# GpSimd makes the first shifted copy of VectorE's exponentials, a fifth key tile for VectorE, LN statistics tile by tile

## The chip, the cores and the metric

One core of a Trainium2 chip runs the whole program. The metric is the device time of one execution in microseconds: 1539.59 as the median of 3 runs (1539.48 to 1539.63).

## The reference

Two layers of attention and MLP with residuals, on x of 2048 rows by 512 columns in bf16; 32 heads of 16 columns, MLP width 1792. Both layers use the same weights.

```python
def _A_ref(x, wqkv, wo):                      # H = 32, Dh = 16
    qkv = (x @ wqkv).reshape(B, S, 3, H, Dh).transpose(2, 0, 3, 1, 4)
    q, k, v = qkv[0], qkv[1], qkv[2]
    scores = jnp.einsum("bhqd,bhkd->bhqk", q, k) * (Dh ** -0.5)
    p = softmax(scores, axis=-1)
    o = jnp.einsum("bhqk,bhkd->bhqd", p, v)
    return o.transpose(0, 2, 1, 3).reshape(B, S, D) @ wo

def _B_ref(x, w1, b1, w2, b2):
    return gelu(x @ w1 + b1) @ w2 + b2

x = x + _A_ref(layernorm(x), wqkv, wo)
x = x + _B_ref(layernorm(x), w1, b1, w2, b2)
x = x + _A_ref(layernorm(x), wqkv, wo)
x = x + _B_ref(layernorm(x), w1, b1, w2, b2)
```

## The kernel before, in words

**Cells.** The queries are taken in four chunks of 512. For one chunk and a group of four heads a *pass* goes over the 16 key tiles of 128 rows. One *cell* is the scores of one key tile, one head and 512 queries: a block of 128x512 in one PSUM bank. There are 2 layers x 32 passes x 16 tiles x 4 heads = 4096 cells. L1234 is their matmul; up to four cells of different heads run side by side in four row groups of TensorE. Its operand `qp` is a masked copy of Q that GpSimd makes (`qpad`, L1182).

**Two engines for exp.** ScalarE takes cells in batches of two or three banks and writes bf16 probabilities into units of the tile `pt`, a ring of PT_RING = 19 (`exps`, L1586). When the ring is full, parts of other tiles that are not in use are lent to it. VectorE takes cells only of the key tiles in KD, four for each layer. Its first pass (`dfirst`, L1386) scales and shifts the scores so that the bits of the uint16 result, read as bf16, approximate exp. Then `dchain` makes three more copies whose bits are shifted by 32, 64 and 96: per pair of cells L1461 writes copy one from copy zero (128x1024), and L1463 writes copies two and three from copies zero and one (128x2048). All four copies go into P·V (L1650), copies one to three against versions of V weighted by VW (`vc`, made by GpSimd in `vcopies`, L1165). So a cell of VectorE needs four P·V matmuls, a cell of ScalarE one. The pairs live in `du`, five buffers, with a sixth over a part of K in layer 1.

Which cells VectorE gets is decided while the program is planned: `attach` adds cells to a score batch where a bank is free, `swap` gives VectorE the third bank of a ScalarE batch when VectorE is less than 0.5 us behind. `next_d` hands out only cells of KD, of this pass and the next. The passes of the first chunk are split by key tiles: in layer 1 twelve passes first go over tiles 0 to 11, and later the same twelve over tiles 12 to 15.

**The rest, in the gaps.** Projections, output projection (`wo`), MLP (`hpair`, `gelu`, `ytile`) and LN run as background work between the cells, some of it released by the number of scores that have been done (`when`). LN takes its statistics on VectorE, rstd on GpSimd (L664, a power), the normalisation on GpSimd (L678, `xln`), and then a DMA transposes the tile (L682) into `xf` (for the MLP) or `xp` (for the next layer's projections). In the last segment LN is normalised on VectorE and transposed on TensorE. TensorE also runs *fillers* (L1222), matmuls whose results nobody reads, only in planned gaps.

**What sets the order.** `_Sched` plays the whole program forward on the host before it is emitted: each engine has a clock, each operation a cost in us, and the next operation of an engine is the ready one with the best priority. The emitted queues keep that order, with semaphore waits for every dependence; the engines then run at their own speed. Costs, latencies and priorities are thus only the plan, but a change of one number can reorder all that follows it. One part of the plan concerns GpSimd and VectorE: the copies of `dchain` are marked `port`, and the plan lets a marked VectorE operation that would begin inside one of the last four GpSimd operations begin only HOLD = 0.4 us later or at that operation's end:

```python
        if op.port and op.eng == "dve":
            at = max(t, self.clock["dve"])
            for a, b in self.pool_ops[-4:]:
                if a < at < b:
                    t = max(t, min(b, at + HOLD))
```

Of the kernel before, what the change touches and what calls it, by code (L numbers as in the profile page):

```python
# [5 lines left out]
ALU = mybir.AluOpType  # L6
# [12 lines left out]
NL = 2  # L19
# [1 line left out]
PVB = 6  # L21
MISC = (7, 5)
THIRD = 5
PT_RING = 19
LEND = (3, 2)
QP_RING = 3
W_RING = 4
# [6 lines left out]
LNP = 7  # L34
# [8 lines left out]
JB = 0.64  # L43
JS = 0.025
EARLY = 4
KD = ((4, 5, 6, 7), (0, 1, 2, 12))
NKD = 4
TAIL = 10
OPENING = 18
ROUNDS = 2  # L50
# [13 lines left out]
CPRIO = 8  # L64
FPRIO = 1.5
PVP = 2
PTURG = 6
DUURG = 1
# [2 lines left out]
DWIDE = 2  # L71
RWIDE = 2
AHEAD = 24
LOG2E = 1.4426950408889634
E_SCALE = 0.25 * LOG2E * 128
E_BIAS = 15992.765054484162
SHIFT = 32
# [128 lines left out]


OWN = 0.022
HOLD = 0.4
LATENCY = {"pe": 0.221, "act": 0.21, "dve": 0.139, "pool": 0.153328, "sp": 0.1}  # L210
OVERLAP = 0.083
ROUND = 1.02

# [1 line left out]
class _Sched:  # L215
# [76 lines left out]
    def _ready(self, op):  # L292
        t = 0.0
        for k in op.reads:
            if k not in self.P.lastw:
                return None
        for ev in self.P.deps(op.reads, op.writes):
            if op.eng == "pe" and ev[0] == "pe":
                continue
            t = max(t, self.end.get(ev, 0.0) - OWN * (op.eng == "dve" == ev[0]))  # L300
        if op.eng == "pe" and op.mode != self.mode:
            t -= SW
        if op.port and op.eng == "dve":
            at = max(t, self.clock["dve"])
            for a, b in self.pool_ops[-4:]:
                if a < at < b:
                    t = max(t, min(b, at + HOLD))
        return t
# [46 lines left out]
    def run(self):  # L355
        while True:
# [21 lines left out]
            for e, cand in best.items():  # L378
# [40 lines left out]
                self.clock[e] = at + MM  # L419
                self.end[ev] = at + MM + LATENCY[e]  # L420
            if e == "pool":
                self.pool_ops.append((start, start + cost))


SW = 0.107
# [111 lines left out]
class _Plan:  # L537
# [109 lines left out]
        yield from self.xmove(h, part(kept, h + 2), home, sem, ["KEPT.%d" % (h + 2)], keys)  # L647
        yield ("give", ("xin", 1, h + 2))

    def ln(self, tiles, dst, dkeys, prio, quick=False):  # L650

        T = self.T
        c, n = tiles[0], len(tiles)
        sl = slice(c, c + n)
        for t in tiles:
            yield ("need", ("xready", t, self.phase[t // 4]))
            yield _Op("dve", 0.66, lambda e, t=t: e.bn_stats(T["STATS"][:, t, :], T["X"][:, t % XT, :]),
                      reads=["X.%d" % (t % XT)], writes=["ST.%d" % t])
# [5 lines left out]
        yield _Op("pool", 0.25 + 0.33 * n, lambda e: e.tensor_tensor(  # L664
            out=T["RSTD"][:, sl], in0=T["VARR"][:, sl], in1=T["NHALF"][:, 0:n], op=ALU.pow),
            reads=["VARR.%d" % c, "NHALF"], writes=["RSTD.%d" % c])
        yield _Op("dve", 0.157, lambda e: e.scalar_tensor_tensor(
            out=T["NMR"][:, sl], in0=T["MV"][:, sl, 0], scalar=-1.0, in1=T["RSTD"][:, sl], op0=ALU.mult, op1=ALU.mult),
            reads=mvk + ["RSTD.%d" % c], writes=["NMR.%d" % c])
        for t in tiles:  # L670
            yield ("spawn", self.ln_tile(c, t, dst, dkeys, quick), prio)

    def ln_tile(self, c, t, dst, dkeys, quick):
        T = self.T
        ph = self.phase[t // 4]
        x = yield ("acq", "xln")
        eng, cost = ("dve", 0.4) if quick else ("pool", 1.0)
# [116 lines left out]
    def norm(self, l, seg, g, b, part, final):  # L794
# [35 lines left out]
        nb = w // 32  # L830
        for i, t in enumerate(ts):
            o3 = T["OTT"][:, o, 0:w].rearrange("p (k c) -> p k c", c=32)[:, :, 16 * t:16 * t + 16]
            yield _Op(*(("pool", 0.1 + 0.62 * w / 512) if pool else ("dve", 0.153 + 0.262 * w / 512)), lambda e, i=i, o3=o3: e.tensor_tensor(  # L833
                out=o3, in0=x3[:, i * nb:i * nb + nb, 0:16],
                in1=T["RC"][:, i * nb:i * nb + nb, None].to_broadcast([128, nb, 16]), op=ALU.mult),
                reads=["XT", "RC"], writes=["OTT.%d.%d" % (o, t)])
# [198 lines left out]
    def post(self, l, seg):  # L1035
# [7 lines left out]
        yield ("need", ("otn", l, seg, 3))  # L1043
        for t in tiles:
            yield ("spawn", self.wo(l, seg, t), 10)
        for t in tiles:
            yield ("need", ("xready", t, 2 * l + 1))
        yield ("give", ("ofree", l, seg))
        self.phase[c] = 2 * l + 1
        if prev:  # L1050
            yield ("need", ("xfree",) + prev)
        xf, xk = lambda t: T["XF"][:, :, (t % 4) * 128:(t % 4) * 128 + 128], lambda t: ["XF.%d" % (t % 4)]
        for ts in ([t] for t in tiles) if last else (tiles,):
            yield ("spawn", self.ln(ts, xf, xk, LNP, last), 0.2 if last else LNP)
        for t in tiles:
            yield ("need", ("lnt", t, 2 * l + 1))
        if prev:
# [10 lines left out]
        for i, t in enumerate(tiles):  # L1068
            yield ("cond", self.when(l, seg, yb + ys * i))
            yield ("spawn", self.ytile(l, seg, t), 13)  # L1070
        for t in tiles:
# [4 lines left out]
        self.phase[c] = 2 * l + 2  # L1076
        if prev:
            yield ("need", ("pfree",) + prev)
        xp, pk = lambda t: T["XP"][:, :, (t % 4) * 128:(t % 4) * 128 + 128], lambda t: ["XP.%d" % (t % 4)]
        yield ("spawn", self.ln(tiles, xp, pk, LNP), LNP)  # L1080
# [90 lines left out]
    def qpad(self):  # L1171
        T = self.T
        for pi, (l, seg, g, kts, part, final) in enumerate(self.pas):
# [5 lines left out]
            s = yield ("acq", "qp")  # L1179
            q = T["Q"][:, b, 512 * qc + q0:512 * qc + q0 + w]  # L1180
            for i, t in enumerate(ts):
                yield _Op("pool", 0.15 + 0.62 * w / 512, lambda e, s=s, q=q, i=i, t=t, w=w: e.tensor_scalar(  # L1182
                    T["QP"][:, s, w * i:w * i + w], q, T["MASK"][:, t:t + 1], 1.0, op0=ALU.mult, op1=ALU.mult),
                    reads=["Q.%d.%d" % (b, qc), "MASK"], writes=["QP.%d" % s])
            yield ("give", ("qp", pi), s)
# [263 lines left out]
    def dchain(self, pair):  # L1449
# [5 lines left out]
        if self.open is pair:  # L1455
# [5 lines left out]
        one = _Op("dve", 0.151 + 0.134 * n, lambda e: e.tensor_scalar(U[:, 1, 0:n, :], U[:, 0, 0:n, :], SHIFT, None, op0=ALU.add),  # L1461
                  reads=key[0], writes=key[1])
        two = _Op("dve", 0.152 + 0.266 * n, lambda e: e.tensor_scalar(U[:, 2:4, 0:n, :], U[:, 0:2, 0:n, :], 2 * SHIFT, None, op0=ALU.add),  # L1463
                  reads=key[0] + key[1], writes=key[2] + key[3])
        one.port = two.port = True
        yield one
        yield two
        self.duleft[du] = n
        for jj, (pi, kt, a) in enumerate(cells):
            l, seg, g = self.pas[pi][:3]  # L1470
# [2 lines left out]
            for i in range(4):  # L1473
                if i == 0:
                    ws, wk = [T["V"][l][:, kt, 8 * gb + 2 * a + t, 0:17] for t in ts], ["V%d.%d" % (l, kt), "V%d1" % l]
                else:
                    ws = [T["VC"][:, j, i - 1, 17 * h:17 * h + 17] for h in [8 * gb + 2 * a + t for t in ts]]
                    wk = ["VC.%d.%d" % (j, i - 1)]
                self.dq[(pi, a)].append((ws, U[:, i, jj, :].bitcast(BF16), wk + [key[i][jj]],
                                         ("du", du) if i == 3 else None, i == 3, kt))  # L1480

    def units(self, n):
        for lo, hi in self.blocks:
# [118 lines left out]
    def pvs(self):  # L1602
        T = self.T
        pools = self.s.pools
        for pi, (l, seg, g, kts, part, final) in enumerate(self.pas):
# [16 lines left out]
                return len(pools["du"]) <= DULOW and len(wide) >= DWIDE and any(self.dq[k] for k in cols)  # L1622

            def urge():
                return 0.5 if len(pools["pt"]) < PTURG or len(pools["du"]) < DUURG else PVP

            def build(op, start, pi=pi, b=b, l=l, cols=cols, begun=begun, n=n):
                op.fns, op.reads, rounds = [], [], 0
# [129 lines left out]
```

## Time and profile before

| | |
|---|---|
| median of 3 runs | 1539.59 us |
| the profiled execution's own time | 1540.0 us |
| its span (first to last instruction) | 1538.2 us |
| ScalarE busy | 1504.6 us, 98% |
| TensorE busy | 1452.2 us, 94% |
| VectorE busy | 1394.3 us, 91% |
| GpSimd busy | 202.9 us, 13% |
| TensorE clock granted | 1.00 |
| chain that ended last, by engine | ScalarE 64%, TensorE 23%, VectorE 12% |

A row of a group names the line, engine and operation, then output and input with shapes and the count; behind the first bar stand the us in which the group kept its engine busy and the mean ns of one instruction, behind the second the idle us just before them and who ended it. Rows of a table by stage give start:end, the length, then busy us and instruction count of PE, PEld, DVE, ACT and POOL, the clock, the DMA share and GB/s. A timeline row gives start, duration, engine, line, operation and count. Instructions of VectorE overlap a little at their ends, so the means of groups add up to more than the busy time. PE is TensorE, DVE VectorE, ACT ScalarE, POOL GpSimd.

### The profile page before, as it was taken

The page shows a single profiled execution, that of the slowest core. Times are in us where ns is not written, and L with a number is a line of the kernel's source. Part 1 is how long each engine was busy: PE and PEld are TensorE (multiplying, and loading weights), DVE is VectorE, ACT ScalarE, POOL GpSimd, SP SyncE. Part 2 cuts the span into 40 slices and gives each one's busy share as a digit, 9 for nine tenths or more (in the row PEclk, how much of TensorE's full clock was granted, in tenths as well). Part 3 has the DMA queues.
Part 4 walks back from the last instruction along what each step waited for, and adds up shares of the span by engine and source line. Part 5 has one row for each costly group of instructions (what it writes and reads, how often), then busy time and mean ns, then how long its engine had stood idle before and what let it go on. Part 6 is the DMA issues. An engine that isn't in the chain of part 4 may idle for free.

```text
span 1538.2 us, 46317 instructions
## 1 busy us (share of the span) xinstructions
PE 1452.2 (94%) x20352; PEld 445.9 (29%) x20352; DVE 1394.3 (91%) x2633; ACT 1504.6 (98%) x1377; POOL 202.9 (13%) x250
## 2 busy tenths in 40 slices
PE   8999899999999999999899999889999999999998
PEld 3222222222222222222222222222222222343344
DVE  6689999989999999989799899899989989999893
ACT  7999999999999999999999999999999999999996
POOL 5300002001020020100320011122002001010000
PEclk9999999999999999999999999999999999999999
DMA  5200001152111531215211431001153105312522
GB/s 145 50 2 1 2 3 42 36 166 84 33 39 50 162 74 36 49 57 157 58 50 43 133 100 46 16 1 36 36 159 91 37 21 163 114 37 69 167 65 64
DMA packets 145045, 103.39 MB, mean 67 GB/s; under 512 B 37069, under 2 KB 143822, under 8 KB 144846
## 3 DMA queue, kind: packets, MB, share of 16 engines
q1 hardware_dynamic: 144846, 100.44, 23.0%
q8 instruction: 162, 2.65, 0.7%
q14 instruction: 37, 0.30, 0.1%
HBM read 88.61 MB, written 4.19 MB: 60 GB/s over the span
## 4 chain that ended last, share of the span: by engine, by line
ACT 64%; PE 23%; DVE 12%; issue 1%; DMA 0%; ACTq 0%; DVEq 0%
ACT pt L1586 57%; PE ps L547 8%; PE ps L1234 7%; PE ps L1650 7%; DVE du L1386 5%; ACT g L986 3%; DVE du L1463 2%; DVE du L1461 1%; ACT kt L1586 1%; ACT v L1586 1%; ACT q L1586 1%; DVE g L965 1%; ACT L1586 1%; ACT L986 1%; DVE kt L1386 0%
## 5 line engine op out<-in xcount | busy, mean ns | idle before, releaser
L1586 ACT ACTIVATE pt<-ps 128x1024 bf16<-128x1024 f32 (+1 forms) x1239 | 1344.8, 1245 | 8.5 <-PE ps L1234 6.5
L1386 DVE TENSOR_SCALAR du<-ps 128x512 uint16<-128x512 f32 x893 | 596.3, 684 | 58.7 <-PE ps L1234 56.2
L1234 PE MATMUL ps<-qp,kt 32*128 32x512 bf16 x4096 | 529.3, 384 | 45.4 <-ACT pt L1586 31.6
L1650 PE MATMUL ps<-pt,v 128*17 128x512 bf16 (+1 forms) x3287 | 405.4, 359 | 13.2 <-ACT pt L1586 8.9
L1650 PE MATMUL ps<-du,vc 128*17 128x512 bf16 (+1 forms) x3000 | 354.5, 358 | 3.6 <-ACT pt L1586 2.0
L1463 DVE TENSOR_SCALAR du<-du 128x2048 uint16<-128x2048 uint16 x448 | 307.9, 694 | 1.7
L1234 PEld LDWEIGHTS ps<-qp,kt 32*128 32x128 bf16 x4096 | 137.4, 91 | 584.0 <-ACT pt L1586 239.9
L1182 POOL TENSOR_SCALAR qp<-q,mask 128x512 bf16<-128x512 bf16 (+1 forms) x91 | 70.9, 779 | 978.6 <-PE ps L1234 968.5
L1461 DVE TENSOR_SCALAR du<-du 128x1024 uint16<-128x1024 uint16 x448 | 183.1, 427 | 2.1
L1650 PE MATMUL ps<-du,v 128*17 128x512 bf16 (+1 forms) x1000 | 162.0, 359 | 7.1 <-DVE xt L823 2.8
L1658 PE MATMUL ps<-vc,zero 128*17 128x512 bf16 x774 | 158.6, 381 | 0.0
L1650 PEld LDWEIGHTS ps<-pt,v 128*17 128x17 bf16 x3287 | 98.9, 88 | 129.7 <-issue 72.9
L547 PE MATMUL ps<-xf,wr 128*32 128x512 bf16 (+1 forms) x1888 | 129.8, 364 | 1.7 <-DVE g L965 1.3
L547 PE MATMUL ps<-wr,g 128*32 128x512 bf16 x1600 | 117.9, 383 | 2.9 <-DVE du L1386 1.0
L1650 PEld LDWEIGHTS ps<-du,vc 128*17 128x17 bf16 x3000 | 95.0, 89 | 80.1 <-issue 43.0
L965 DVE TENSOR_SCALAR g<-ps,hb1t 128x512 bf16<-128x512 f32 (+1 forms) x112 | 79.7, 712 | 2.4 <-PE ps L547 2.4
L1222 PE MATMUL ps<-vc 128*32 128x512 bf16 x852 | 68.1, 382 | 0.9 <-DVE du L1386 0.7
L678 POOL TENSOR_SCALAR xln<-x,rstd,nmr 128x512 bf16<-128x512 bf16 x58 | 55.3, 956 | 41.5 <-DMA xf<-xln 15.0
L1650 PEld LDWEIGHTS ps<-du,v 128*17 128x17 bf16 x1000 | 41.7, 89 | 51.9 <-issue 18.1
L1386 DVE TENSOR_SCALAR kt<-ps 128x512 uint16<-128x512 f32 x81 | 55.5, 685 | 1.2 <-PE ps L1234 0.9
L1222 PE MATMUL ps<-vc,zero 128*17 128x512 bf16 x692 | 56.4, 382 | 0.0
L833 POOL TENSOR_TENSOR ott<-xt,rc 128x256 bf16<-128x256 f32 x42 | 32.2, 767 | 174.5 <-DVE rc L826 150.4
(90 smaller groups left out, 1077.4 us busy)
## 6 DMA issues: line engine op xcount, KB each, us to landing
wr<-in_B_w_dram SPq DMA_DIRECT2D x256, 256.0 KB, 2.8
wr<-in_A_wqkv_dram SPq DMA_DIRECT2D x24, 256.0 KB, 3.0
wr<-in_A_wo_dram SPq DMA_DIRECT2D x18, 256.0 KB, 3.1
x<-in_A_x_dram SPq DMA_DIRECT2D x7, 512.0 KB, 4.4
kept<-x SPq DMA_DIRECT2D x4, 512.0 KB, 2.9
x<-kept SPq DMA_DIRECT2D x4, 512.0 KB, 4.0
out_dram<-x SPq DMA_DIRECT2D x16, 128.0 KB, 2.8
g<-in_A_wqkv_dram SPq DMA_DIRECT2D x3, 512.0 KB, 5.5
```

The source lines that it names most:

```text
L547: return [lambda e, a=a: e.matmul(out[32 * a:32 * a + 32, :], lhsT=lhsT[:, 32 * a:32 * a + 32], rhs=rhs, start=start, stop=stop, tile_posi ...
L965: yield _Op("dve", 0.21 + n / 966, lambda e, fc=fc, pb=pb: e.tensor_scalar(T["G"][:, fc, q], pb, T["HB1T"][:, fc:fc + 1], None, op0=ALU.ad ...
L986: lambda e, g=g: e.activation(out=g, in_=g, func=ACT.Gelu_apprx_tanh), reads=gk, writes=gk, prio=2)
L1182: yield _Op("pool", 0.15 + 0.62 * w / 512, lambda e, s=s, q=q, i=i, t=t, w=w: e.tensor_scalar(T["QP"][:, s, w * i:w * i + w], q, T["MASK"] ...
L1222: fns.append(lambda e, o=o, w=w, a=a, m=m: e.matmul(o, lhsT=w, rhs=rhs, start=start, stop=start, tile_position=(0, m * a)))
L1234: return (lambda e: e.matmul(o, lhsT=lhsT, rhs=rhs, start=True, stop=True, tile_position=(32 * a, 0)), ["K%d.%d.%d" % (l, gb, kt // 4), "Q ...
L1386: yield _Op("dve", 0.682, lambda e: e.tensor_scalar(u, self.bank(b), E_SCALE, E_BIAS, op0=ALU.mult, op1=ALU.add), reads=["B.%d" % b], writ ...
L1461: one = _Op("dve", 0.151 + 0.134 * n, lambda e: e.tensor_scalar(U[:, 1, 0:n, :], U[:, 0, 0:n, :], SHIFT, None, op0=ALU.add), reads=key[0], ...
L1463: two = _Op("dve", 0.152 + 0.266 * n, lambda e: e.tensor_scalar(U[:, 2:4, 0:n, :], U[:, 0:2, 0:n, :], 2 * SHIFT, None, op0=ALU.add), reads ...
L1586: yield _Op("act", 0.065 + 0.4267 * n, lambda e, src=src, dst=dst: e.activation(out=dst, in_=src, func=ACT.Exp, scale=0.25), reads=["B.%d" ...
L1650: op.fns.append(lambda e, o=o, lhsT=q[0][0][m], rhs=q[0][1][:, n * m:n * m + n], a=a, st=st, sp=sp: e.matmul(o, lhsT=lhsT, rhs=rhs, start= ...
L1658: op.fns.append(lambda e, o=self.bank(b)[32 * a:32 * a + 17, :], rhs=rhs, a=a, st=not begun[a], sp=end: e.matmul(o, lhsT=T["ZERO"][:, 0:17 ...
```

## The change

*Copies.* In `dchain`, if the planned clock of GpSimd is at most PSHIFT = 2 us ahead of VectorE's, copy one becomes an add on GpSimd (`dpool`), and VectorE makes copies two and three as two instructions of 128x1024 straight from copy zero; otherwise VectorE does all as before. The pair is handed to P·V when all three have been planned.

*Key tiles.* KD has five tiles for each layer; `vc` grows by three copies of V, and the ring `pt` shrinks from 19 units to 15.

*LN.* The statistics are started as soon as a tile of the residual is there, ahead of the wait for `xf` or `xp` to be free; that wait now stands before the normalisation (`gate`). The LN behind the first layer's MLP works in two halves of two tiles.

*The plan.* HOLD falls to 0.06, and a GpSimd operation is planned longer by half of the time that it shares with a marked VectorE copy; costs of GpSimd operations and one latency change; P·V gets priority 0.3 when all scores are done.

```diff
-PT_RING = 19
+PT_RING = 15
-KD = ((4, 5, 6, 7), (0, 1, 2, 12))
-NKD = 4
+KD = ((4, 5, 6, 7, 8), (0, 1, 2, 12, 13))
+NKD = 5
+PSHIFT = 2
-HOLD = 0.4
-LATENCY = {"pe": 0.221, ...
+HOLD = 0.06
+EXTEND = 0.5
+LATENCY = {"pe": 0.219, ...
...
             if e == "pool":
-                self.pool_ops.append((start, start + cost))
+                self.pool_ops.append([start, start + cost, ev])
+            if e == "dve" and op.port and self.pool_ops:
+                last = self.pool_ops[-1]
+                both = min(start + cost, last[1]) - max(start, last[0])
+                if both > 0:
+                    last[1] += EXTEND * both
+                    self.clock["pool"] = last[1]
+                    self.end[last[2]] += EXTEND * both
...  # ln
-    def ln(self, tiles, dst, dkeys, prio, quick=False):
+    def ln(self, tiles, dst, dkeys, prio, quick=False, gate=None):
-        yield _Op("pool", 0.25 + 0.33 * n, ...
+        yield _Op("pool", 0.37 + 0.18 * n, ...
...
+        if gate:
+            yield ("need", gate)
         for t in tiles:
             yield ("spawn", self.ln_tile(c, t, dst, dkeys, quick), prio)
...  # post
         for t in tiles:
             yield ("spawn", self.wo(l, seg, t), 10)
+        self.phase[c] = 2 * l + 1
+        xf, xk = ...
+        gate = ("xfree",) + prev if prev else None
+        for ts in ([t] for t in tiles) if last else (tiles,):
+            yield ("spawn", self.ln(ts, xf, xk, LNP, last, gate), 0.2 if last else LNP)
         for t in tiles:
             yield ("need", ("xready", t, 2 * l + 1))
         yield ("give", ("ofree", l, seg))
-        self.phase[c] = 2 * l + 1
-        if prev:
-            yield ("need", ("xfree",) + prev)
-        ...
...
+        if l < NL - 1:
+            self.phase[c] = 2 * l + 2
+            xp, pk = ...
+            for ts in (tiles[:2], tiles[2:]):
+                yield ("spawn", self.ln(ts, xp, pk, LNP, gate=("pfree",) + prev if prev else None), LNP)
         for t in tiles:
             yield ("need", ("xready", t, 2 * l + 2))
...  # dchain
-        yield one
-        yield two
+        flat = [U[:, i, 0:n, :].rearrange("p j q -> p (j q)") for i in range(4)]
+        if self.s.clock["pool"] <= self.s.clock["dve"] + PSHIFT:
+            yield ("spawn", self.dpool(pair, flat, key, n), CPRIO)
+            for i in (2, 3):
+                op = _Op("dve", 0.151 + 0.134 * n, lambda e, i=i: e.tensor_scalar(flat[i], flat[0], SHIFT * i, None, op0=ALU.add),
+                         reads=key[0], writes=key[i])
+                op.port = True
+                yield op
+            yield ("cond", lambda: pair.get("copied"))
+        else:
+            one = ...  # as before
+            two = ...  # as before
+            yield one
+            yield two
...
+    def dpool(self, pair, flat, key, n):
+        yield _Op("pool", 0.15 + 0.536 * n, lambda e: e.tensor_scalar(flat[1], flat[0], float(SHIFT), 1.0, op0=ALU.add, op1=ALU.mult),
+                  reads=key[0], writes=key[1])
+        pair["copied"] = True
...  # pvs
-                return 0.5 if len(pools["pt"]) < PTURG or len(pools["du"]) < DUURG else PVP
+                return 0.3 if self.ended else 0.5 if len(pools["pt"]) < PTURG or len(pools["du"]) < DUURG else PVP
```

More of the change, by code (lines that the diff above doesn't have):

```diff
@@ L208 @@
 OWN = 0.022
-HOLD = 0.4
-LATENCY = {"pe": 0.221, "act": 0.21, "dve": 0.139, "pool": 0.153328, "sp": 0.1}
+HOLD = 0.06
+EXTEND = 0.5
+LATENCY = {"pe": 0.219, "act": 0.21, "dve": 0.139, "pool": 0.153328, "sp": 0.1}
 OVERLAP = 0.083
@@ L304, in _ready @@
             at = max(t, self.clock["dve"])
-            for a, b in self.pool_ops[-4:]:
+            for a, b, _ in self.pool_ops[-4:]:
                 if a < at < b:
@@ L663, in ln @@
                   reads=mvk, writes=["VARR.%d" % c])
-        yield _Op("pool", 0.25 + 0.33 * n, lambda e: e.tensor_tensor(
+        yield _Op("pool", 0.37 + 0.18 * n, lambda e: e.tensor_tensor(
             out=T["RSTD"][:, sl], in0=T["VARR"][:, sl], in1=T["NHALF"][:, 0:n], op=ALU.pow),
@@ L676, in ln_tile @@
         x = yield ("acq", "xln")
-        eng, cost = ("dve", 0.4) if quick else ("pool", 1.0)
+        eng, cost = ("dve", 0.4) if quick else ("pool", 0.77)
         yield _Op(eng, cost, lambda e: e.tensor_scalar(
@@ L832, in norm @@
             o3 = T["OTT"][:, o, 0:w].rearrange("p (k c) -> p k c", c=32)[:, :, 16 * t:16 * t + 16]
-            yield _Op(*(("pool", 0.1 + 0.62 * w / 512) if pool else ("dve", 0.153 + 0.262 * w / 512)), lambda e, i=i, o3=o3: e.tensor_tensor(
+            yield _Op(*(("pool", 0.63 * w / 512) if pool else ("dve", 0.153 + 0.262 * w / 512)), lambda e, i=i, o3=o3: e.tensor_tensor(
                 out=o3, in0=x3[:, i * nb:i * nb + nb, 0:16],
@@ L1045, in post @@
             yield ("spawn", self.wo(l, seg, t), 10)
+        self.phase[c] = 2 * l + 1
+        xf, xk = lambda t: T["XF"][:, :, (t % 4) * 128:(t % 4) * 128 + 128], lambda t: ["XF.%d" % (t % 4)]
+        gate = ("xfree",) + prev if prev else None
+        for ts in ([t] for t in tiles) if last else (tiles,):
+            yield ("spawn", self.ln(ts, xf, xk, LNP, last, gate), 0.2 if last else LNP)
         for t in tiles:
@@ L1048, in post @@
         yield ("give", ("ofree", l, seg))
-        self.phase[c] = 2 * l + 1
-        if prev:
-            yield ("need", ("xfree",) + prev)
-        xf, xk = lambda t: T["XF"][:, :, (t % 4) * 128:(t % 4) * 128 + 128], lambda t: ["XF.%d" % (t % 4)]
-        for ts in ([t] for t in tiles) if last else (tiles,):
-            yield ("spawn", self.ln(ts, xf, xk, LNP, last), 0.2 if last else LNP)
         for t in tiles:
@@ L1070, in post @@
             yield ("spawn", self.ytile(l, seg, t), 13)
+        if l < NL - 1:
+            self.phase[c] = 2 * l + 2
+            xp, pk = lambda t: T["XP"][:, :, (t % 4) * 128:(t % 4) * 128 + 128], lambda t: ["XP.%d" % (t % 4)]
+            for ts in (tiles[:2], tiles[2:]):
+                yield ("spawn", self.ln(ts, xp, pk, LNP, gate=("pfree",) + prev if prev else None), LNP)
         for t in tiles:
@@ L1075, in post @@
             return
[L1076 to L1080, printed above, removed]
         for t in tiles:
@@ L1181, in qpad @@
             for i, t in enumerate(ts):
-                yield _Op("pool", 0.15 + 0.62 * w / 512, lambda e, s=s, q=q, i=i, t=t, w=w: e.tensor_scalar(
+                yield _Op("pool", 0.27 + 0.42 * w / 512, lambda e, s=s, q=q, i=i, t=t, w=w: e.tensor_scalar(
                     T["QP"][:, s, w * i:w * i + w], q, T["MASK"][:, t:t + 1], 1.0, op0=ALU.mult, op1=ALU.mult),
@@ L1460, in dchain @@
         key = [["DU.%d.%d.%d" % (du, i, j) for j in range(n)] for i in range(4)]
[L1461 to L1465, printed above, removed]
-        yield one
-        yield two
+        flat = [U[:, i, 0:n, :].rearrange("p j q -> p (j q)") for i in range(4)]
[8 more added lines that the diff above has]
+        else:
+            one = _Op("dve", 0.151 + 0.134 * n, lambda e: e.tensor_scalar(flat[1], flat[0], SHIFT, None, op0=ALU.add),
+                      reads=key[0], writes=key[1])
+            two = _Op("dve", 0.152 + 0.266 * n, lambda e: e.tensor_scalar(U[:, 2:4, 0:n, :], U[:, 0:2, 0:n, :], 2 * SHIFT, None, op0=ALU.add),
+                      reads=key[0] + key[1], writes=key[2] + key[3])
+            one.port = two.port = True
+            yield one
+            yield two
         self.duleft[du] = n
@@ L1480, in dchain @@
                                          ("du", du) if i == 3 else None, i == 3, kt))
+    def dpool(self, pair, flat, key, n):
+        yield _Op("pool", 0.15 + 0.536 * n, lambda e: e.tensor_scalar(flat[1], flat[0], float(SHIFT), 1.0, op0=ALU.add, op1=ALU.mult),
+                  reads=key[0], writes=key[1])
+        pair["copied"] = True
     def units(self, n):
```

## The prediction

> **What bounds the kernel now.** I read the engine shares of the page first, then a table of three stages, then the costliest groups, the waits, and last the timeline where VectorE and GpSimd meet. From the page:
>
> ```profile
> PE 1452.2 (94%) x20352; PEld 445.9 (29%) x20352; DVE 1394.3 (91%) x2633; ACT 1504.6 (98%) x1377; POOL 202.9 (13%) x250
> ```
>
> The table by stage (opening, middle, closing; busy us of each engine):
>
> ```profile
> 0.00:77.00 77.00, 71.47 (x877) 21.83 (x877) 46.71 (x101) 68.70 (x70) 33.34 (x54) 1.00 0.37 97
> 77.00:1463.00 1386.00, 1311.57 (x17983) 387.51 (x17981) 1298.44 (x2425) 1375.97 (x1247) 165.85 (x191) 1.00 0.23 66
> 1463.00:1538.20 75.20, 69.17 (x1498) 36.54 (x1494) 49.17 (x109) 59.90 (x62) 3.71 (x5) 1.00 0.23 66
> ```
>
> In the middle ScalarE is busy 1375.97 of 1386 us (99.3%), VectorE 1298 (93.7%), TensorE 1312 (94.6%), at clock 1.00. ScalarE sets the pace; the time falls only where exponentials leave it. What they cost:
>
> ```profile
> L1586 ACT ACTIVATE pt<-ps 128x1024 bf16<-128x1024 f32 (+1 forms) x1239 | 1344.8, 1245 | 8.5 <-PE ps L1234 6.5
> L1386 DVE TENSOR_SCALAR du<-ps 128x512 uint16<-128x512 f32 x893 | 596.3, 684 | 58.7 <-PE ps L1234 56.2
> L1463 DVE TENSOR_SCALAR du<-du 128x2048 uint16<-128x2048 uint16 x448 | 307.9, 694 | 1.7
> L1461 DVE TENSOR_SCALAR du<-du 128x1024 uint16<-128x1024 uint16 x448 | 183.1, 427 | 2.1
> ```
>
> A cell (one 128x512 block of scores) goes to ScalarE (L1586) or to VectorE: a first pass from PSUM (L1386), then per pair of cells L1461 and L1463. With the `kt` rows VectorE has 893 + 81 = 974 of 4096 cells. The list allows 2 layers x 32 passes x 4 key tiles x 4 = 1024, so it is nearly used up. The waits of VectorE in the middle agree:
>
> ```profile
> DVE du L1386 <- PE ps L1234: 54.2, 71, 4.0
> ```
>
> 54 of its 88 idle us it waits for a cell to be given. A fifth tile raises the ceiling to 1280.
>
> The dispute is the copies. First VectorE, then GpSimd, in one window:
>
> ```profile
> 1280.04 0.69 DVE L1018 TENSOR_TENSOR x<-x,ps 128x512 bf16<-128x512 bf16 x1
> 1280.64 0.69 DVE L1386 TENSOR_SCALAR du<-ps 128x512 uint16<-128x512 f32 x1
> 1281.24 0.69 DVE L1463 TENSOR_SCALAR du<-du 128x2048 uint16<-128x2048 uint16 x1
> 1281.84 0.76 DVE L1461 TENSOR_SCALAR du<-du 128x1024 uint16<-128x1024 uint16 x2
> 1282.51 1.30 DVE L1463 TENSOR_SCALAR du<-du 128x2048 uint16<-128x2048 uint16 x2
> ```
>
> ```profile
> 1280.85 3.30 POOL L1182 TENSOR_SCALAR qp<-q,mask 128x256 bf16<-128x256 bf16 x2 [17.09 <-PE ps L1234]
> ```
>
> Instructions of 0.69 us start every 0.60 us, two copies of 128x1024 take 1282.51 - 1281.84 = 0.67, so 0.335 each. Meanwhile two GpSimd operations that take 0.48 each in undisturbed rows need 3.30: the row of copies keeps GpSimd out. The other way round:
>
> ```profile
> 1190.45 0.85 DVE L1461 TENSOR_SCALAR kt<-kt 128x1024 uint16<-128x1024 uint16 x1
> ```
>
> ```profile
> 1190.05 0.96 POOL L833 TENSOR_TENSOR ott<-xt,rc 128x256 bf16<-128x256 f32 x1 [1.47 <-DVE rc L826]
> ```
>
> A copy of 0.42 that begins inside a GpSimd operation takes 0.85. Counted over the whole trace: of 968 full copies 89 begin inside a GpSimd operation; 28 of them wait, 0.30 us on average, so 0.095 over all 89. Of the other 879 one is late.
>
> **Part by part.** All sums are for the middle stage, W = 1386 us; opening and closing (152 us) stay.
>
> *VectorE, before.* Two first passes and both copies: 2 x 0.60 + 0.335 + 0.60 = 2.135 us a pair, 1.07 a cell. 944 first passes start in the middle: 1008 us. The rest (residuals, bias, LN, norms) is 1298 - 1008 = 290.
>
> *VectorE, after.* Two separate 128x1024 copies replace one of 1024 and one of 2048: 2 x 0.60 + 2 x 0.335 = 1.87, a saving of 0.265 a pair, 0.935 a cell, before any wait. The wait is the unknown. GpSimd's 1024-column add stands in no row. Its q padding takes 0.48 at 256 columns and 0.69 at 512 when undisturbed, so 0.69 + 2 x 0.21 = 1.1 us; twice the 512 row is 1.4; I take 1.2. A blocked copy waited at most 0.43 behind the 0.69 operation, so about 0.94 behind this one. Bounds of the wait per pair: 0 (copies two and three follow the first pass on their own engine, GpSimd needs a semaphore and then queues behind them, as at 1280.85) and 0.94. GpSimd would be busy 203 + 500 x 1.4 = 900 us, 60%; two copies x 0.6 x 0.095 = 0.11, more for an operation twice as long. I take 0.15, near the low end, because the order within a pair favours VectorE. One pair in ten, where GpSimd is planned over 2 us late, stays at the old price. Cell: 0.9 x (0.935 + 0.075) + 0.1 x 1.07 = 1.016.
>
> The Trainium skill (SBUF — State Buffer, "Who interferes with whom") has a rule that speaks against the change: VectorE in a two-port mode and GpSimd hold the shared port pair for a whole instruction, and whoever issues second is fully blocked. The two windows above agree with it in both directions; the average of 0.095 says that it seldom falls on VectorE here. What it would cost is the second rival.
>
> *ScalarE.* In the middle it does 3823 - 944 = 2879 cells in 1323 us, 0.46 a cell; at 99.3% busy a moved cell is worth 0.463 of W.
>
> *The sum.* n cells go to VectorE, which reaches 96.5% (the best stages of 77 us reach 75 to 76, 98%; 34 of the 88 idle us are not for want of cells): n = (0.965 W - 290) / 1.016, W = 1386 - 0.463 (n - 944). This gives W = 1358, n = 1004: 60 cells more, 28 us less. Span 1538.2 - 28 = 1510. The profiled execution took 1540.0, 1.8 above its span, and the median is 0.4 lower: 1512.
>
> *TensorE.* A moved cell brings three more matmuls; 3788 of them on `du` cost 411 us in the middle, 0.109 each: 60 x 3 x 0.109 = 20 us, against 74 us idle and the fillers (L1222, 117 us of rows), which are placed only into gaps. Fewer ScalarE batches also mean fewer score rounds. I take nothing; without that cover 20 us.
>
> *GpSimd's queue.* The extra `vc` copies are 2 x 3 x 0.65 = 4 us; tile 8's V is written at 55.8, the first pair starts at 65.2. q padding and LN's `xln` now queue behind up to two or three adds, 2 to 4 us. q padding has waited 968 us in total for a buffer, so it is early. The first FFN matmul of a chunk follows its last `xln` by 5 to 7 us in the trace, so FFN, with the 58 transposes that SP's queue issues after `xln`, would come some 3 us later; it is background work, and no ScalarE batch in the middle waited for it. Nothing; 3 us if the last segment is held up by it.
>
> *LN.* The same 64 statistics, earlier and spread out on VectorE's queue; four groups become eight, with four more variance and `nmr` steps (0.19 and 0.15 us each, under 1.5 us of VectorE) and four more powers on GpSimd. At the end it could start 0.6 us sooner, but the chain there is TensorE's from 1514.5 to 1535.4. Nothing, or 0.6 gained.
>
> *Ring of 15 instead of 19.* ScalarE fills a unit in 0.46 us, so TensorE may lag 6.9 us, not 8.7. L1586 is idle 8.5 us in all, nearly all on scores, none seen for a unit. Nothing; up to 8 us if TensorE lags. The planner's new costs move every instruction a little; I bound that by the 10 us ScalarE idles in the middle, either way.
>
> **The rivals.**
>
> *The locks never meet.* VectorE alternates 1.2 us of first passes, which leave GpSimd alone (843 first passes without overlap and 131 with it both average 684 ns), and two copies; GpSimd's add fits into the first passes. Cell 0.935, VectorE 97.5%: W = 1326, time 1480. Against it: first passes and copies of several pairs come mixed, as above.
>
> *The lock turns on VectorE (slower).* GpSimd lags, its add for one pair still runs when the next pair's copies are due, and everything behind them on VectorE waits: first passes, so the third bank of a ScalarE batch. At half a hold, 0.47 a pair, a cell costs 1.17: W = 1402, time 1556. It decides from a wait of 0.35 a pair (cell 1.11, W = 1386). For it: 28 of 89, counted under a planner that puts a copy off by up to HOLD = 0.4 when GpSimd is planned busy, which the change lowers to 0.06; against it: VectorE starts first. With GpSimd always first, 0.94 a pair would give 1609 (an estimate). That is what the rule of the Trainium skill named above would make of this order; the windows shown hold both orders.
>
> *Copy one comes late to TensorE (slower).* It is done some 2 us after the first pass instead of 0.4; TensorE takes its queue in order, scores stand behind that matmul, ScalarE runs dry. If one pair in ten loses 0.8 us: 52 x 0.8 = 41, time 1553. It decides from 28 us over 517 pairs, 0.05 each.
>
> *The copies bring nothing, only the fifth tile does* (few adds reach GpSimd, or a wait of 0.27 eats the saving): cell 1.07, 96.5%: W = 1374, time 1527.
>
> **How the numbers follow.** Forecast 0.51 (its own range 1495 to 1524), locks never meet 0.17, tile alone 0.10, lock on VectorE 0.14, late copy 0.08. About 0.2% (3 us) is what a measurement of this kernel can tell from no change. Faster is the first three less 0.03 that would end within it, 0.75; slower is the last two less 0.01, 0.21; same 0.04. The range leaves out half of the best case and half of the two slower ones, some 0.2: 1482 to 1552.
>
> **What would show it.** Right: about 1030 first passes in all, GpSimd 50 to 65% busy with adds of 1.2 to 1.8 us, copies of 128x1024 at a mean of 0.43 to 0.50, VectorE at 94% of the whole span or more, ScalarE still at 98%. The lock: copies at a mean of 0.60 or more. The late copy: ScalarE idle above 60 us, and TensorE waiting on GpSimd's `du`. Tile alone: GpSimd under 40%. I am wrong if ScalarE's share falls below 96%, or if first passes stay under 990.

## The result, and the profile after

1630.97 us (median of 4 runs, 1626.4 to 1634.3) against 1539.53 before: ratio 1.059, 95% interval 1.0577 to 1.0602. The forecast was 1512, the range 1482 to 1552. The profiled execution took 1626.4 us, its span 1624.6.

The engine shares of the changed kernel's page:

```profile
PE 1472.5 (91%) x20210; PEld 441.8 (27%) x20210; DVE 1503.8 (93%) x2787; ACT 1507.6 (93%) x1374; POOL 797.1 (49%) x786
```

Its table by stage, with the middle lengthened by the 86 us that the span grew:

```profile
0.00:77.00 77.00, 71.77 (x916) 22.46 (x916) 46.78 (x102) 67.96 (x69) 38.08 (x60) 1.00 0.38 97
77.00:1549.00 1472.00, 1331.96 (x17810) 383.23 (x17806) 1402.02 (x2565) 1381.11 (x1245) 735.65 (x705) 1.00 0.22 62
1549.00:1624.60 75.60, 68.76 (x1496) 36.07 (x1488) 55.04 (x122) 58.56 (x62) 23.35 (x22) 1.00 0.23 67
```

Opening and closing are much as before. In the middle VectorE is busy 95.2% (93.7 before), ScalarE 93.8% (99.3 before). ScalarE no longer sets the pace, although it has fewer cells: the groups of the page show 961 + 87 = 1048 first passes instead of 974, and what the copies now cost:

```profile
L1611 ACT ACTIVATE pt<-ps 128x1024 bf16<-128x1024 f32 (+1 forms) x1110 | 1213.7, 1173 | 77.9 <-PE ps L1244 66.1
L1503 POOL TENSOR_SCALAR du<-du 128x1024 uint16<-128x1024 uint16 (+1 forms) x482 | 548.4, 1138 | 586.7 <-DVE du L1396 571.4
L1396 DVE TENSOR_SCALAR du<-ps 128x512 uint16<-128x512 f32 x961 | 635.9, 674 | 41.2 <-PE ps L1244 39.6
...
L1475 DVE TENSOR_SCALAR du<-du 128x1024 uint16<-128x1024 uint16 (+1 forms) x964 | 539.3, 586 | 2.8
```

A copy of 128x1024 takes 586 ns in the mean, not 427. The add (L1503) is at 1138 close to the 1.2 us that was assumed. And ScalarE now sits idle 66 us for scores (6.5 before). What the scores wait for, from the waits, before and after:

```profile
PEld ps L1234 <- ACT pt L1586: 239.9, 487, 1.9
...
PEld ps L1234 <- DVE du L1386: 116.4, 272, 1.1
```

```profile
PEld ps L1244 <- DVE du L1396: 231.9, 451, 1.6
...
PEld ps L1244 <- ACT pt L1611: 145.0, 309, 1.8
```

TensorE waits twice as long for a first pass of VectorE to free a bank, and less for ScalarE. The chain that ended last turns over with it: VectorE 73%, ScalarE 8% (12 and 64 before).

Where the copies lose the time, VectorE and then GpSimd in one window of the changed kernel's timeline:

```profile
533.33 1.28 DVE L1396 TENSOR_SCALAR du<-ps 128x512 uint16<-128x512 f32 x2
534.53 1.60 DVE L1475 TENSOR_SCALAR du<-du 128x1024 uint16<-128x1024 uint16 x2
536.05 0.67 DVE L1396 TENSOR_SCALAR du<-ps 128x512 uint16<-128x512 f32 x1
```

```profile
534.70 1.15 POOL L1503 TENSOR_SCALAR du<-du 128x1024 uint16<-128x1024 uint16 x1 [0.38 <-DVE du L1396]
```

The add begins 0.17 us after the first copy of the row, and the row takes 1.60 instead of 0.75: copy three starts 0.335 us after copy two, but takes 1.60 - 0.335 = 1.27 us instead of 0.42 and ends only behind the add. The 0.85 us more are its *wait*. Counted over the trace: of 1044 full copies 335 begin inside an add, 296 of these wait, 0.55 us each, 163 us in all; with the other GpSimd operations 178 us, 0.34 a pair. 120 of the 296 are the second copy of a row, as here.

### The profile page after: what moved, and what is told of

The parts are those of the page before. It is cut to its first block, busy times and chain, and to the rows that moved or that the text cites. A ratio compares the mean times of both kernels' runs of the same rounds, so it can differ in the third digit from the quotient of the medians.

```text
span 1624.6 us, 46908 instructions
## 1 busy us (share of the span) xinstructions
PE 1472.5 (91%) x20210; PEld 441.8 (27%) x20210; DVE 1503.8 (93%) x2787; ACT 1507.6 (93%) x1374; POOL 797.1 (49%) x786
## 4 chain that ended last, share of the span: by engine, by line
DVE 73%; PE 16%; ACT 8%; issue 1%; DMA 0%; POOL 0%; DVEq 0%; ACTq 0%
DVE du L1396 30%; DVE du L1475 24%; ACT pt L1611 6%; PE ps L556 6%; PE ps L1244 5%; PE ps L1675 5%; DVE g L976 3%; DVE kt L1396 3%; DVE kt L1475 2%; DVE stats L666 1%; DVE xt L834 1%; DVE x L1029 1%; DVE otn L853 1%; DVE x L881 1%; ACT g L997 1%
## 5 line engine op out<-in xcount | busy, mean ns | idle before, releaser
L1611 ACT ACTIVATE pt<-ps 128x1024 bf16<-128x1024 f32 (+1 forms) x1110 | 1213.7, 1173 | 77.9 <-PE ps L1244 66.1
L1503 POOL TENSOR_SCALAR du<-du 128x1024 uint16<-128x1024 uint16 (+1 forms) x482 | 548.4, 1138 | 586.7 <-DVE du L1396 571.4
L1396 DVE TENSOR_SCALAR du<-ps 128x512 uint16<-128x512 f32 x961 | 635.9, 674 | 41.2 <-PE ps L1244 39.6
L1475 DVE TENSOR_SCALAR du<-du 128x1024 uint16<-128x1024 uint16 (+1 forms) x964 | 539.3, 586 | 2.8
L1675 PE MATMUL ps<-pt,v 128*17 128x512 bf16 (+1 forms) x2867 | 382.0, 360 | 8.9 <-ACT pt L1611 2.6
L1683 PE MATMUL ps<-vc,zero 128*17 128x512 bf16 x728 | 153.2, 382 | 0.0
L1675 PEld LDWEIGHTS ps<-du,vc 128*17 128x17 bf16 x3243 | 99.9, 89 | 99.3 <-issue 50.3
L1611 ACT ACTIVATE kt<-ps 128x1024 bf16<-128x1024 f32 (+1 forms) x85 | 99.2, 1177 | 6.0 <-PE ps L1244 2.1
L1611 ACT ACTIVATE v<-ps 128x1024 bf16<-128x1024 f32 (+1 forms) x73 | 81.9, 1151 | 5.3 <-PE ps L1244 2.9
L1503 POOL TENSOR_SCALAR kt<-kt 128x1024 uint16<-128x1024 uint16 (+1 forms) x44 | 48.3, 1097 | 54.2 <-DVE kt L1396 52.7
L1675 PE MATMUL ps<-kt,v 128*17 128x512 bf16 (+1 forms) x308 | 73.5, 367 | 1.0 <-DVE xt L834 0.9
```

The lines of the kernel that those rows point to most:

```text
L1396: yield _Op("dve", 0.682, lambda e: e.tensor_scalar(u, self.bank(b), E_SCALE, E_BIAS, op0=ALU.mult, op1=ALU.add), reads=["B.%d" % b], writ ...
L1475: op = _Op("dve", 0.151 + 0.134 * n, lambda e, i=i: e.tensor_scalar(flat[i], flat[0], SHIFT * i, None, op0=ALU.add), reads=key[0], writes= ...
L1503: yield _Op("pool", 0.15 + 0.536 * n, lambda e: e.tensor_scalar(flat[1], flat[0], float(SHIFT), 1.0, op0=ALU.add, op1=ALU.mult), reads=key ...
L1611: yield _Op("act", 0.065 + 0.4267 * n, lambda e, src=src, dst=dst: e.activation(out=dst, in_=src, func=ACT.Exp, scale=0.25), reads=["B.%d" ...
L1675: op.fns.append(lambda e, o=o, lhsT=q[0][0][m], rhs=q[0][1][:, n * m:n * m + n], a=a, st=st, sp=sp: e.matmul(o, lhsT=lhsT, rhs=rhs, start= ...
L1683: op.fns.append(lambda e, o=self.bank(b)[32 * a:32 * a + 17, :], rhs=rhs, a=a, st=not begun[a], sp=end: e.matmul(o, lhsT=T["ZERO"][:, 0:17 ...
```

## The experiments

The theory: while GpSimd's add runs, VectorE's copies wait for it (**lock**), and the plan, with HOLD at 0.06, does not see it (**blind plan**). The rivals: the fifth tile, the ring of 15 or LN; and copy one coming late to TensorE. "Waits" are counted as above, over all GpSimd operations.

| run | first passes | waits, us | VectorE, ScalarE busy | us | ratio to before (95%) |
|---|---|---|---|---|---|
| changed kernel | 1048 | 178 | 93, 93% | 1631.0 | 1.0577-1.0602 |
| e1 narrow add | 1048 | 15 | 89, 97 | 1518.7 | 0.9848-0.9878 |
| e2 no add | 1009 | - | 93, 97 | 1545.0 | 1.0021-1.0046 |
| e3 add after copies | 1030 | 150 | 90, 92 | 1628.1 | 1.0560-1.0592 |
| e4 add alone | 966 | 102 | 89, 98 | 1546.6 | 1.0030-1.0060 |
| e5 HOLD 0.9 | 978 | 64 | 88, 97 | 1551.7 | 1.0067-1.0099 |
| e6 blind, four tiles | 982 | 181 | 89, 93 | 1648.8 | 1.0693-1.0725 |
| e7 fifth tile alone | 1003 | - | 92, 97 | 1540.0 | 0.9993-1.0013 |
| e8 LN alone | 964 | - | 90, 98 | 1545.1 | 1.0026-1.0052 |
| e9 e6 with HOLD 0.4 | 970 | 93 | 89, 98 | 1548.2 | 1.0035-1.0068 |
| e11 add in halves | 962 | 77 | 88, 98 | 1545.4 | 1.0022-1.0048 |
| e12 add alone, HOLD 0.9 | 958 | 67 | 87, 98 | 1549.3 | 1.0044-1.0074 |
| e13 HOLD 0.4 | 1002 | 95 | 91, 97 | 1549.2 | 1.0044-1.0074 |
| e16 halves, five tiles | 985 | 81 | 89, 97 | 1545.1 | 1.0020-1.0046 |
| e17 scalar from a tile | 1048 | 129 | 91, 94 | 1593.4 | 1.0326-1.0361 |
| e18 e13 and e17 | 1002 | 56 | 89, 97 | 1539.5 | 0.9986-1.0004 |
| e10, e14, e15 controls | 970 each | - | 90, 97-98 | 1547.6, 1544.0, 1547.5 | 1.0015 to 1.0068 |

### e1: the lock taken away, plan and order kept

The add covers 32 of its 1024 columns, so this kernel leaves out nearly all of copy one.

```diff
-    e.tensor_scalar(flat[1], flat[0], float(SHIFT), 1.0, ...
+    e.tensor_scalar(flat[1][:, 0:32], flat[0][:, 0:32], float(SHIFT), 1.0, ...
```

> The changed kernel with its plan and the order of all engines kept; only GpSimd's add is cut from 1024 columns to 32 (the rest of copy one keeps an old value; the buffers are filled once by GpSimd in the opening). Theory 'lock' (VectorE's copies wait while GpSimd's add runs: in the changed kernel 335 of 1044 copies of 128x1024 begin inside an add and lose 163 us): the copies fall from a mean of 587 to about 430 ns, VectorE's busy time by 140 to 170 us, and ScalarE sets the pace again: 1485 to 1520 us. Theory 'rest of the change' (fifth tile's extra matmuls, the ring of 15, LN's order): no change, 1610 to 1635. Theory 'late copy one' (TensorE waits for GpSimd): faster too, but with VectorE's copies still at 550 ns or more.

1518.7 us, within the 1485 to 1520 of the lock. The groups of this run:

```profile
L1611 ACT ACTIVATE pt<-ps 128x1024 bf16<-128x1024 f32 (+1 forms) x1110 | 1192.2, 1219 | 6.4 <-PE ps L1675 3.1
...
L1475 DVE TENSOR_SCALAR du<-du 128x1024 uint16<-128x1024 uint16 (+1 forms) x964 | 386.3, 429 | 2.8
```

Same instructions in the same order, copies back at 429 ns, ScalarE's idle time before a batch down from 77.9 to 6.4 us, VectorE 156 us less busy. The rest of the change, which is all still there, can't be the cause, and with hardly any add and 15 us of waits the plan gains 1.4%, near the 1.8% that was forecast.

### e2 to e4: parts of the change

e2 sets PSHIFT to -1e9, so that VectorE makes all copies. e3 makes the add wait for the pair's own copies:

```diff
-            yield ("spawn", self.dpool(...), CPRIO)      # ahead of copies two and three
+            yield ("spawn", self.dpool(...), CPRIO)      # behind copies two and three
...
-                  reads=key[0], writes=key[1])
+                  reads=key[0] + key[2] + key[3], writes=key[1])
```

e4 puts the new copies into the kernel before, all else as it was.

> The changed kernel with VectorE making all copies in the two old instructions (the condition for GpSimd never holds); fifth tile, ring of 15, LN and the new costs of the plan stay; the plan is made anew. 'Lock': 1515 to 1540 us, copies at 420 and 690 ns. 'Rest of the change': 1600 or more. 'Late copy one': as 'lock'.

> The changed kernel with GpSimd's add of a pair made to wait for the pair's own two copies on VectorE, so that it can only run into copies of other pairs; copy one is ready later by about 0.7 us. 'Lock': fewer copies begin inside an add (200 to 280 instead of 335), 1575 to 1615 us. 'Late copy one': slower than the changed kernel, above 1640, and TensorE's waits for GpSimd above 40 us (9.5 us in the changed kernel). 'Rest of the change': as the changed kernel, 1620 to 1640.

> The kernel before with GpSimd's add and the two separate copies alone: four key tiles, ring of 19, LN and plan (HOLD 0.4) as before. 'Lock': slower than before, 1555 to 1600 us, copies at a mean of 500 ns or more. 'Rest of the change': 1505 to 1540. 'Late copy one': 1550 to 1600, with TensorE waiting on GpSimd's du for 40 us or more.

e2 (1545.0) missed by 5 us, since 1515 to 1540 was expected: without the add the other parts cost 0.3%, not 5.9. e3 missed: the waits fall only from 178 to 150 us, since the add meets copies of other pairs, and the time hardly moves. Its 1628 is what the rest of the change would give too, but e1 and e2 rule that out. e3 refutes the late copy, which asked for over 1640 and for long waits of TensorE on GpSimd's `du`; TensorE waits 32 us for it in e3 and 9.5 in the changed kernel. e4 missed on the good side (1546.6, not 1555 to 1600): the add with all its lock costs 0.45% under the old plan. So the lock alone is not 5.9%; something in the new plan is needed.

### e5, e6, e9, e13: the number that makes the plan blind

e5: the changed kernel with HOLD = 0.9; e13 with HOLD = 0.4. e6: the whole new plan with the add, but four tiles, ring of 19 and old LN; e9: e6 with HOLD = 0.4.

> The changed kernel with one number of its plan: HOLD 0.9 instead of 0.06, so that the plan puts a copy that would begin inside a GpSimd operation off to that operation's end (at most 0.9 us) and does something else first. Theory 'blind plan' (the lock alone costs VectorE some 170 us, but the 5.9% come from a plan that does not know it: it hands VectorE 1048 cells and orders TensorE and ScalarE by copies that come late): under 1010 first passes, copies at a mean of 450 to 520 ns, ScalarE at 96% or more, 1530 to 1560 us. Theory 'lock alone' (the wait cannot be planned around): 1590 or more.

> GpSimd's add with the whole new plan (HOLD 0.06, GpSimd operations stretched by half an overlap, new costs, the new priority at the end) but four key tiles, ring of 19 and LN as before; it differs from the run of the add alone by the plan's numbers only. 'Blind plan': some 1000 first passes, copies at 560 ns or more, 1565 to 1610 us. 'Fifth tile' (with four tiles VectorE cannot be given too much): as the add alone, 1540 to 1555.

> The run with the blind plan and four key tiles (1648.8 us) with HOLD back at 0.4 and nothing else changed. If HOLD is the number that makes the plan blind: 1543 to 1560, waits of the copies halved from 181 us. If it is the stretching of GpSimd's operations, the new costs or the new priority at the end: 1600 or more.

> The changed kernel with HOLD back at its old value 0.4 and nothing else changed (1551.7 us at 0.9, 1631 at 0.06). 'Blind plan': 1540 to 1560 us, waits of the copies at half of 163 us or less. If the fifth tile needs the longer HOLD: 1565 or more.

The engine shares of e6 and of e9, which differ by that one number:

```profile
PE 1482.2 (90%) x20252; PEld 446.7 (27%) x20252; DVE 1459.7 (89%) x2651; ACT 1528.8 (93%) x1369; POOL 755.5 (46%) x745
```

```profile
PE 1453.7 (94%) x20400; PEld 445.7 (29%) x20400; DVE 1373.0 (89%) x2623; ACT 1508.3 (98%) x1374; POOL 741.6 (48%) x737
```

HOLD from 0.06 to 0.4 gives back 100.7 of e6's 109 us over before (e9), and 81.8 of the changed kernel's 91 (e13); at 0.9 (e5) it gives back 79. All three times came out as the blind plan had forecast. The waits about halve (181 to 93, 178 to 95 us). At the 0.7 to 0.8 us of time per us of wait that e1 and e17 show, this is worth 60 to 70 us; the rest would come with the new order, but no run separates it. e6 missed upwards (1565 to 1610 expected), and it corrects the theory in one respect: VectorE had not been given too much. It has 982 first passes, 8 more than before, and no engine is full. VectorE is late, and the others wait in turn. TensorE waits for first passes, and ScalarE for scores, in e6 and then in e9:

```profile
PEld ps L1243 <- DVE du L1395: 207.7, 404, 2.0
ACT pt L1610 <- PE ps L1243: 80.7, 154, 2.8
```

```profile
PEld ps L1243 <- DVE du L1395: 69.4, 164, 0.8
ACT pt L1610 <- PE ps L1243: 5.7, 18, 0.8
```

### e7, e8 and the controls e10, e14, e15

e7: five tiles and ring of 15 alone. e8: LN alone. The controls change one assumed latency of the plan, no work:

```diff
-LATENCY = {"pe": 0.221, "act": 0.21, "dve": 0.139, ...
+LATENCY = {"pe": 0.219, ...          # e10; 0.223 in e14; "dve": 0.141 in e15
```

> The kernel before with five key tiles and the ring of 15 alone; VectorE makes all copies, LN and plan as before. By the working of the prediction VectorE goes from 93.7 to 96.5% of the middle and takes some 20 to 30 cells more: 1525 to 1535 us. 'Ceiling is not the limit' (in the run without the add 1009 first passes did not make it faster): 1538 to 1550.

> The kernel before with the new LN alone (statistics started tile by tile, halves behind the first MLP; costs of the plan as before). By the prediction nothing: 1537 to 1541. If LN's order explains the 0.3% that the run without the add lost: 1543 to 1547.

> A control: the kernel before with one number of the plan changed, the latency assumed for TensorE 0.219 instead of 0.221. It removes no work and adds none. If any new plan costs a few tenths of a per cent (LN alone 0.4%, fifth tile without the add 0.3%): 1541 to 1547 us. If those two are effects of their own: 1538 to 1541.

> Second control: the kernel before with TensorE's assumed latency 0.223 instead of 0.221. If any new plan costs a few tenths of a per cent: 1542 to 1550. If the first control was an accident of 0.219: 1538 to 1541.

> Third control: the kernel before with VectorE's assumed latency 0.141 instead of 0.139. As the second control: 1542 to 1550, or 1538 to 1541.

The fifth tile moves 29 cells and no time (1540.0, not 1525 to 1535). LN alone costs 0.4%, but so does a latency that removes nothing: 0.26 to 0.51% in three controls. A new order of the same work is worth that much here. All three controls lose; whether the plan of before is an unusually good one, so that any new plan starts some us behind it, is not shown. So the losses of LN, of e2, e4, e9, e12 and e13 can't be told from it, and whether they have causes of their own stays open.

### e11, e12, e16: versions that avoid the lock

e11: the add alone in two GpSimd instructions of 512 columns, HOLD 0.45. e16: the same with five tiles and ring of 15. e12: the add alone with HOLD 0.9.

> The add alone in the kernel before (1546.6 us), but GpSimd makes it in two instructions of 128x512, planned at 1.24 us, and HOLD is 0.45: if the lock is held for one instruction, a copy waits at most some 0.45 us instead of 0.85, so the mean of the copies falls from 521 to 460 to 490 ns and the time to 1532 to 1544. If the lock is not given up between the two: as the add alone, 1544 to 1550.

> The add alone in the kernel before (1546.6 us) with HOLD 0.9 instead of 0.4: the plan keeps copies out of GpSimd's whole operation. 'Blind plan': copies at a mean of 450 to 490 ns instead of 521, 1530 to 1545 us. 'Lock alone': 1545 or more, because the time that the copies are put off is lost all the same.

> The add in two halves with HOLD 0.45 (1545.4 us with four tiles, VectorE 88% busy and waiting 92 us for cells), with five key tiles and the ring of 15, LN as before. If cells are what VectorE lacks: some 1020 first passes, 1525 to 1537. If TensorE or the plan takes it back, as with the fifth tile alone: 1538 to 1552.

e11 missed 1532 to 1544, and its copies of 499 ns the 460 to 490. The longest waits halve (95 of 100 copies take under 0.84 us, 1.27 in e4), so the lock is given up between the two instructions, but more copies begin inside one (232 against 193): 77 us of waits instead of 102, and 1.2 us of time. e12 cuts the waits to 67 us and gains nothing either: 1549.3, not 1530 to 1545, where 'lock alone' had put it. e16 got 985 first passes, not 1020, and the time of e11. In the four-tile runs with HOLD at 0.4 or more ScalarE is back at 98%, so VectorE's time is no longer what counts.

### e17, e18: who gets the lock

In the changed kernel a GpSimd operation that begins during the first of two copies in a row blocks the second behind the add in 120 of 124 cases, `vc` 3 of 3, the norm's tensor_tensor 16 of 17; behind the q padding 1 of 16, `xln` 0 of 15. The last two take one or both of their numbers from a tile. e17 keeps plan and order and gives the add its 32 from a tile:

```diff
-    e.tensor_scalar(flat[1], flat[0], float(SHIFT), 1.0, ...
+    e.tensor_scalar(flat[1], flat[0], self.T["SH"][:, 0:1], 1.0, ...
```

> The changed kernel with its plan and the order of all engines kept; only the 32 that GpSimd's add adds comes from a tile of 128x1 float32 (filled in the opening) instead of standing in the instruction, as the q padding and xln take theirs. Theory 'the form decides' (an operation that first fetches its scalar asks for the lock later, so a row of VectorE's copies keeps it): the second copy of a row waits in under 20% of the cases instead of 120 of 124, the waits of the copies fall from 163 to under 90 us, the add itself gets longer (1.3 us or more instead of 1.13), 1520 to 1575 us. Rival 'length decides' (the add wins because it is longer): no change, 1620 to 1635 us.

VectorE and GpSimd in one window of e17:

```profile
594.40 0.75 DVE L1475 TENSOR_SCALAR du<-du 128x1024 uint16<-128x1024 uint16 x2
595.07 0.68 DVE L770 CAST v<-ps 128x512 bf16<-128x512 f32 x1
```

```profile
594.58 1.48 POOL L1503 TENSOR_SCALAR du<-du,sh 128x1024 uint16<-128x1024 uint16 x1 [0.97 <-DVE du L1396]
```

The add again begins 0.18 us into the row, but now the row takes 0.75 and the add 1.48: 0 of 122 second copies wait. The form decides who gets the lock there, not the length. 113 us of waits behind the add remain, not under 90, of copies that begin well inside one, so the time (1593.4) is 38 us better and missed the 1520 to 1575. GpSimd itself is busier than in the changed kernel (862.7 against 797.1 us) and the time still falls, so its load, which the prediction weighed for q padding and LN, is not the main cost.

e18 is e13 with this form:

> The changed kernel with HOLD 0.4 and with the add's scalar taken from a tile; plan and order of all engines as in the run with HOLD 0.4 (1549.2 us, copies at 511 ns). If the two cures add up: copies at 450 to 480 ns, 1530 to 1544 us. If, as in the other runs with a plan that sees the lock, VectorE is no longer what is late: 1544 to 1552.

1539.5 us, 10 us better than e13 in the same order, as the first forecast had it: waits 56 us, copies at 474 ns. It ties with the kernel before (interval 0.9986 to 1.0004). No version that makes all copies beats it; e1 shows about what the lock withholds.

## Why the prediction was wrong

**Right.** ScalarE as the bound of before, and the add's duration (1.14 against 1.2 us). The longest hold, put at 0.94, was measured at 0.85. TensorE hardly waited for copy one (9.5 us). Partly luck is that e1, at 1518.7, lies near the 1512: the sum had 0.15 us of waits a pair in it, and with e1's 0.03 it gives about 1494, a saving of 46 us where e1 shows 21.

**The first wrong term: the wait per pair, 0.15 us, measured 0.34.** It took 0.6 of the copies as beginning inside a GpSimd operation, at 0.095 us each. Inside an add it was 335 of 1044, 0.32, but at 163 / 335 = 0.49 us each. The 0.095 was a mean over all GpSimd operations, from 89 copies. Split by form, the same trace of before had 0.33 us over the 9 copies that began inside the norm's tensor_tensor or a `vc` copy, and 0.08 over the 71 inside q padding or `xln`. The add has the form of `vc`, numbers in the instruction; its row, not the mean, was the nearest. The reason given for the low end, that copies two and three are ahead of GpSimd within the pair, was read from 1280.85, a q padding. With the add the second copy of the row loses (120 of 124). The rule of the Trainium skill (SBUF — State Buffer, "Who interferes with whom") that the second to issue is fully blocked agrees with the copy above that ends only behind the add. The same section of the Trainium skill says that issue order decides who blocks, and not the shape of the operation; at the seam between two copies this does not foretell the winner, since by the recorded starts the add comes ahead of the second copy both in the changed kernel and in e17 (by 0.17 and 0.16 us in the windows shown), and e17 turned the outcome around by the form of one number alone.

**The second: a sum in which the cells go where there is time.** With 0.34 the sum still gives about 1538 us, because n shrinks as a cell gets dearer, so the wait explains only 26 of the 119 us between forecast and result. But n is fixed when the program is planned. With the measured 1010 first passes of the middle, at (1.87 + 0.34) / 2 = 1.105 us a cell, and 96.5%, it is W = (290 + 1010 x 1.105) / 0.965 = 1457, against 1472 measured. This fits the changed kernel, yet e6 shows that it is not the mechanism: with 951 first passes in the middle and 181 us of waits the same sum gives about 1404, measured 1494. What is missing is the lateness: an unplanned wait on VectorE holds a bank, then a score, then ScalarE, as the waits of e6 show (208 and 80.7 us). In the runs that keep one order the time follows the waits at 0.7 to 0.8: e1 163 us less wait, 112 less time; e17 49 and 38. Under a plan that sees the lock it is 0.25: e18 against e13 39 and 10.

**The rival was there, with the wrong price.** "The lock turns on VectorE" named place and mechanism, and that HOLD falls to 0.06 stood in it as a reason; the 1556 took the same elastic n. Its chance of 0.14 leaned on 28 of 89. Its sign, copies at 0.60 or more, was nearly met at 0.586. ScalarE's idle time above 60 us, put down as a sign of the late copy, came with the lock instead.

**Smaller terms.** The fifth tile alone was put at 1527 and is 1540.0: it moved 29 cells, VectorE reached 92%, and ScalarE fell to 97%; that TensorE's extra work cost nothing was likely wrong, since its share of the chain that ended last rises from 23 to 37% in e7 (whose profiled execution, at 1545.0 us, is the slowest of its ten), but no run isolates it. LN, put at nothing, is within the spread of the controls. TensorE's clock, 0.989 to 0.996 over the four runs of the changed kernel, is too little to matter: these runs lie within 8 us of each other.

## What to carry to other kernels

Where the order is fixed by a plan, cost an edit at that order: a wait that the plan does not know is paid in time by every engine behind it (here 0.7 to 0.8 us for each us), and no work moves away to make up for it. Take the price of a contention from rows of the same form of instruction, not from a mean over all that share the port. Before reading anything into a few tenths of a per cent, change a number of the plan that does no work and see how far the time moves.

## What the runs showed of the hardware

Who gets the lock at the seam between two VectorE copies in a row depends on the form of GpSimd's instruction. With both numbers in the instruction it takes the lock (120 of 124 in the changed kernel, 75 of 76 in e13); with one scalar read from a tile it does not (0 of 122 in e17, 0 of 76 in e18), and GpSimd's operation waits for the row instead: 1.48 us in the window shown, against about 1.12 undisturbed in e17; the other form takes 1.04 undisturbed. The other operations of the changed kernel fall in line, the norm's tensor_tensor (16 of 17) with the first form; the small power that makes rstd (128x4 at most), a tensor_tensor too, held up none of the 18 copies that began inside it. Why is not shown; the 0.08 us between the undisturbed durations would fit a later request.
